# Block pairs of a fused attention and two-MLP kernel: the weight ring moved by 32 bytes, the sums given to VectorE in a new order, and the second token loads issued later

## The chip, the cores and the metric

The kernel runs on one core of a Trainium2 chip. A core has a matrix engine (TensorE, PE in the rows; its weight loads are listed apart as PEld), a vector engine (VectorE, DVE), a scalar engine (ScalarE, ACT), GpSimd (POOL), and SyncE (SP), which here issues all DMA transfers, one after the other in the program's order. The metric is the time of one execution on the device in microseconds (us), as the median of several runs. A change under about 0.2% can't be told from none.

## The reference

Attention is computed twice through 32 packed queries per head, and its output goes through two MLPs. The change touches the second MLP alone.

```python
def _attn_ref(q, k, v, p):
    scale = 1.0 / np.sqrt(q.shape[-1])
    def sm_attn(qq, kk, vv):
        s = scale * np.matmul(qq, kk.transpose(0, 1, 3, 2))
        ...
        return np.matmul(a, vv)
    p_packed = sm_attn(p, k, v)
    return sm_attn(q, p_packed, p_packed)          # 8 x 8 heads, 576 tokens, 64

def _moe_ref(x, w_in, w_out):                      # 4608 x 512, 512 x 2048, 2048 x 512
    h = x @ w_in
    return ((h - np.tanh(h)) @ w_out)

def _moe2_ref(x, w_in, w_out):                     # the same shapes
    h = x @ w_in
    return ((h * np.cos(h)) @ w_out)
```

## The kernel before

A float32 product is made of three reduced-precision products: each operand is split into a `hi` part (rounded by ScalarE) and a `lo` part (the difference, by VectorE), and TensorE computes hi x hi, lo x hi and hi x lo. The result of the first MLP is stored transposed in DRAM as `y1`.

The second MLP works on blocks of 512 tokens (`TB`). The first three are computed plainly (lines 626 and 687). The other six are taken in three pairs (`for t in pairs`, line 1301), and a pair is computed by Strassen-like products of 2x2 blocks: seven products instead of eight, with sums of blocks before and after. A pair has two stages.

- **h blocks.** `F` runs over 8 groups of 256 hidden columns. Each block makes seven products `hprod` (line 883, six matmuls of 512 columns each), with weights of the ring `hw` (`hs.get()`, 8 tiles of 256 KB) and token sums `b` as the moving operand. The names are `B11`, `T1`, `T2`, `B21`, `B22`, `T3`, `T4`. The results stand in three PSUM banks A, C and B of a rotation of four. ScalarE copies intermediate values out (`c1`, `c5`, `c2`), VectorE adds them into `ha` and `hb`, then come rounding, sine and the product with h for the cosine, by `e_round`, `e_frac`, `e_sin`, `e_b2`, `e_a2`, `e_l`, `e_s`, which also leave the operands `K` of the second stage. In the first block of the first pair the weights come from `wf`, tiles that were loaded ahead into another pool. Block F also makes the direct products of block F-1 (`ychunk`): four pieces of six matmuls of 256 columns (line 893), which wait in the list `pend`, and `pop()` issues one piece at a chosen place.
- **Products.** 20 jobs (`jobs`, five kinds `p` in the order `YORDER`, four parts `P` each) of 24 matmuls of 256 columns (line 893): the activations are the weights, and the moving operand is the ring `yw` (5 tiles of 256 KB). For each job ScalarE and VectorE split its operand into `yh` and `yl` (`ysplit`), three jobs ahead. Some operands need a difference of `K` tiles first: `psub`, two per part, 24 in all, on GpSimd. The last job is cut into four pieces that go to `pend` and are issued in the next pair's first blocks.

While the products of a pair run, the token sums of the next pair are prepared by `bprep` (line 815): 26 steps, 13 for each half `j` of the channels. Step 0 and step 13 each load two tiles of 512 KB from `y1` (line 824); the others subtract (line 832, on GpSimd in the pairs), round to `hi` (line 845, 860) and split to `lo` (line 848, 863). The table `PREP` says after which job each step is issued. The loads go into the tiles `gh` and `gl`, two of each, so that the second half's tiles are those of the first half.

The order on each engine is that of the source here (a manual schedule). SP issues the loads of both rings, the token loads and the stores in one queue. A ring load waits for its tile's last matmul, a token load for the last reader of its tile, and everything behind it in the queue waits as well.

Of the kernel before, what the change touches and what calls it, by code (L numbers as in the profile page):

```python
# [10 lines left out]
F32 = mybir.dt.float32  # L11
# [8 lines left out]
ALU = mybir.AluOpType  # L20
# [31 lines left out]
PREP1 = {  # L52
    18: (0,), 19: (1, 2, 5), 20: (3, 4, 13), 21: (6, 7, 8, 9, 14, 15, 18), 22: (10, 16, 17, 19, 20),
    24: (24, 25),
}
# [6 lines left out]
HOPS = ("A11", "S1", "S2", "A12", "S4", "S3", "A22")  # L62
YORDER = (7, 6, 4, 5, 3)
AHEAD = (4, 6)
S4AT = (5, 7, 9, 10)
PREP = {
    0: (0,), 1: (1, 2, 5), 4: (3, 4), 5: (6, 7), 6: (8, 9, 13), 7: (10,), 8: (14, 15, 18), 9: (11, 12),
    10: (16, 17), 11: (19, 20), 12: (21, 22), 13: (23,), 15: (24, 25),
}
SGN = -2147483648  # L70
LOW_BIAS = -0.5 + 2.0 ** -10

# [2 lines left out]
def fused_kernel(ctx, tc, qT, kT, v, pT, w1i, w1o, w2i, w2o, ident, out):  # L75
    nc = tc.nc
    B, _, _, _, HB = qT.shape
# [21 lines left out]
    op = dram.tile([2, 4, 128, DM], F32, name="op")  # L99
# [15 lines left out]
    def f32(ap):  # L115
        return ap.bitcast(F32)
# [10 lines left out]
    class Conv:  # L127
# [47 lines left out]
        def b_ops(self):  # L175
# [5 lines left out]
            def sign():  # L181
                nc.vector.scalar_tensor_tensor(
                    out=x, in0=hi, scalar=SGN, in1=x, op0=ALU.bitwise_and, op1=ALU.bitwise_or
                )
# [448 lines left out]
    def pt2(tag, dt=F32):  # L633
        return p2.tile([128, 2, TB], dt, tag=tag, bufs=2, name=tag)
# [244 lines left out]
    def hprod(dst, w, b, first):  # L879
        n = 0  # L880
        for wi, bi in ((0, 0), (1, 0), (0, 1)):
            for j in range(2):
                nc.tensor.matmul(  # L883
                    out=dst, lhsT=w[:, wi, 128 * j:128 * j + 128], rhs=b[j][bi],
                    start=(first and n == 0), stop=(n == 5), skip_group_check=True,
                )
                n += 1
# [12 lines left out]
    def vec(out, x, y, op=ALU.add):  # L900
        nc.vector.tensor_tensor(out=out, in0=x, in1=y, op=op)  # L901
# [221 lines left out]
    pend, hist, bo, nyt, sums, loaded, evacs = [], [], {}, [], [], [], []  # L1123
# [14 lines left out]
    for n, (i, t, s, a, b) in enumerate(seq):  # L1138
# [9 lines left out]
        for k, x in enumerate(sums):  # L1148
            y = []
# [37 lines left out]
    p4 = p2x["r"]  # L1187
# [14 lines left out]
    def pop(n=1):  # L1202
        for _ in range(n):
            if pend:
                pend.pop(0)()
            while evacs:
                evacs.pop(0)()
# [6 lines left out]
    ha, hb, aa, ab = ea["h"], eb["h"], ea["a"], eb["a"]  # L1214
    spare = [big("ka"), big("kb")]

    banks = [psx.tile([128, TB], F32, tag=f"p{i}", bufs=1, name="p") for i in range(4)]
    nbank = [2]

# [52 lines left out]
    K, kind = {}, {7: 3, 6: 3, 4: 22, 5: 1, 3: 12}  # L1272
# [18 lines left out]

    def ysplit(p, P):
        both = ysplit_lo(*ysplit_hi(p, P))
        if p == 7:
            psub(K[3, P], K[22, P], K[3, P])
        return both

    def psub(o, x, y):
        nc.gpsimd.tensor_tensor(out=o, in0=x, in1=y, op=ALU.subtract)  # L1299

    for t in pairs:
        last = t == pairs[-1]
        Y = {}
        K.clear()

        def e_b2(F):
            vec(ab[:, 0], ab[:, 0], hb[:, 0], ALU.mult)
            vec(ktile(22, F), ab[:, 1], hb[:, 1], ALU.mult)
            vec(ktile(1, F), ktile(22, F), ab[:, 0])

        def e_a2(F, g):
            vec(aa, aa, ha, ALU.mult)
            g["h"], g["l"] = pt2("gh", F32R), pt2("gl", F32R)
            cp(g["h"], aa)
            cp(ktile(12, F), aa[:, 1])

        def e_l(g):
            vec(g["l"], aa, f32(g["h"]), ALU.subtract)

        def e_s(F):  # L1320
            vec(ktile(3, F), aa[:, 0], ab[:, 0], ALU.subtract)

        jobs = [(p, P) for p in YORDER for P in range(NSTEP // 2)]
        done = []
        for F in range(NSTEP):
            w = wfirst if (t, F) == (pairs[0], 0) else None

            def wn(i):
                return w[i] if w else hs.get()

            A, C, B = psp(), psp(), psp()
            c1, c5, c2 = ct("c1"), ct("c5"), ct("c2")
            g = {}
            hprod(A, wn(0), bo["B11"], True)
            hprod(C, wn(1), bo["T1"], True)
            cp(c1, A)
            if F:
                e_sin(eb)
                pop()
            hprod(A, wn(2), bo["T2"], False)  # L1340
            hprod(B, wn(3), bo["B21"], True)
            cp(c5, C)
            if F:
                e_sin(ea)
                e_b2(F - 1)
            cp(c2, A)
            if w:
                for i in PREP1[24]:
                    prep[i]()
            if F:  # L1350
                e_a2(F - 1, g)
            vec(ha[:, 0], B, c1)
            if F:
                e_s(F - 1)
            if F in AHEAD:
                ahead = ysplit_hi(7, len(done))
            hprod(C, wn(4), bo["B22"], False)
            vec(hb[:, 0], C, c2)
            hprod(A, wn(5), bo["T3"], False)
            vec(hb[:, 1], A, c5)  # L1360
            pop(2 if F else 1)
            if F:
                e_l(g)
                while late:
                    late.pop(0)()
                pend.extend(ychunk(Y, F - 1, g["h"], g["l"]))
            put_due()
            hprod(A, wn(6), bo["T4"], False)
            e_round(eb)
            cp(ha[:, 1], A)  # L1370
            if F in AHEAD:
                P = len(done)
                done.append(ysplit_lo(*ahead))
                psub(K[3, P], K[22, P], K[3, P])
            e_round(ea)
            e_frac(eb)
            e_frac(ea)
            pop()
        g = {}
        e_sin(eb)  # L1380
        e_b2(NSTEP - 1)
        e_sin(ea)
        done.append(ysplit(7, 2))
        e_a2(NSTEP - 1, g)
        pop(len(pend))
        e_l(g)
        e_s(NSTEP - 1)
        pend.extend(ychunk(Y, NSTEP - 1, g["h"], g["l"]))
        bo, prep = {}, []
        if not last:  # L1390
            qtags = iter(("gh", "gl", "gh", "gl", "gh", "gl"))
            prep = bprep(
                t + 2, bo, lambda j, nm: pt2(next(qtags)), nc.gpsimd
            )
        Cy = [psp(), psp()]
        for k, (p, P) in enumerate(jobs):
            if k == 3:
                pop(len(pend))
                cp(ha[:, 0], Y["A"][0], TWO_PI)
                cp(ha[:, 1], Y["A"][1], TWO_PI)  # L1400
                plus(ha, Y["B"], ha)
                put(t, 0, 0, ha)
            dst = Y["B"] if p == 3 else Y["A"] if p in (5, 6) else Cy
            hi, lo = done[k]
            fresh = p in (7, 3) and P == 0
            if k == len(jobs) - 1:
                wy = {}

                def tail(half, x, hi=hi, lo=lo, wy=wy, dst=dst):
                    if x not in wy:  # L1410
                        wy[x] = ys.get()
                    yprod(dst, hi[:, x], lo[:, x], wy[x], (2 * half, 2 * half + 1), False)

                def ctail(dst=dst, t=t, o=u2):
                    plus(o, dst, o)
                    put(t, 0, 256, o)

                order = [(h, x) for h in range(2) for x in range(2)]
                pend.extend(lambda h=h, x=x, tail=tail: tail(h, x) for h, x in order)
                late.append(ctail)  # L1420
            else:
                for x in range(2):
                    yprod(dst, hi[:, x], lo[:, x], ys.get(), range(4), fresh and x == 0)
            put_due()
            if len(done) < len(jobs):
                done.append(ysplit(*jobs[len(done)]))
            if k in S4AT:
                i = S4AT.index(k)
                psub(K[12, i], K[12, i], K[3, i])
            if prep:  # L1430
                for i in PREP.get(k, ()):
                    prep[i]()
            if P == NSTEP // 2 - 1:
                if p == 7:
                    cp(hb[:, 0], Cy[0], TWO_PI)
                    cp(hb[:, 1], Cy[1], TWO_PI)
                elif p == 6:
                    cp(aa[:, 0], Y["A"][0], TWO_PI)
                    cp(aa[:, 1], Y["A"][1], TWO_PI)
                elif p == 4:  # L1440
                    plus(aa, Cy, aa)
                    put(t, 1, 0, aa)
                elif p == 5:
                    u2 = [otile(0), otile(1)]
                    cp(u2[0], Y["A"][0], TWO_PI)
                    cp(u2[1], Y["A"][1], TWO_PI)
                    plus(hb, Y["A"], hb)
                    put(t, 1, 256, hb)
# [57 lines left out]
```

## Time and profile before

| | |
|---|---|
| median of 3 runs | 1549.1 us (1548.79 to 1551.68) |
| the profiled execution | 1547.2 us, of which the span from first to last instruction is 1545.2 us |
| TensorE busy | 1478.7 us, 96% of the span |
| VectorE busy | 1216.0 us, 79% |
| ScalarE busy | 976.5 us, 63% |
| GpSimd busy | 250.8 us, 16% |
| mean granted TensorE clock | 0.978 of 2.4 GHz |
| the three pairs | from 1043.6 us on; products end at 1211.9, 1378.2 and 1541.4 us |

The profile lists each instruction with its start and duration, and for idle time before one the instruction that ended it. Matmuls are pipelined: one of 512 columns is listed with 389 ns and the next starts some 230 ns later, so the time from start to start is what it costs. An engine's busy share says little by itself; what counts is where TensorE waits, and for whom.

### The profile page before, as it was taken

How to read it: one execution, taken by the hardware profiler on the slowest of the kernel's cores; microseconds unless marked ns; L12 is line 12 of the kernel's file. 1: busy time of each engine (PE TensorE's matmuls, PEld its weight loads, DVE VectorE, ACT ScalarE, POOL GpSimd, SP SyncE). 2: the span in 40 equal slices, each digit the busy share in tenths (PEclk: the TensorE clock that was granted, in tenths of full speed). 3: DMA queues.
4: the chain of work that ended last, by engine and by line, in shares of the span. 5: the costliest groups of instructions: out<-in, count | busy, mean ns of one | idle time of the engine just before them, and what ended most of it. 6: DMA issues, size and time to landing. Idle time of an engine off the chain costs nothing. (4 is left out here: it accounts for less than half of the span.)

```text
span 1545.2 us, 28227 instructions
## 1 busy us (share of the span) xinstructions
PE 1478.7 (96%) x11056; PEld 1323.5 (86%) x11056; DVE 1216.0 (79%) x1625; ACT 976.5 (63%) x1512; POOL 250.8 (16%) x147
## 2 busy tenths in 40 slices
PE   4879999999999999999999999999998999899999
PEld 1669888999899999989977788888888888898898
DVE  5999888787878878788956558877889578957884
ACT  6878656666656667578867656655665366536652
POOL 1221110010101001011223410000017001630140
PEclk6789999999999999999999999999999999999999
DMA  9523222111112111114658868956666766776656
GB/s 351 190 73 115 82 88 84 47 61 38 60 63 66 63 57 41 48 32 163 200 194 280 278 228 288 356 198 202 188 209 194 215 199 185 219 211 200 181 151 183
DMA packets 149188, 242.56 MB, mean 157 GB/s; under 512 B 12288, under 2 KB 93184, under 8 KB 149056
## 3 DMA queue, kind: packets, MB, share of 16 engines
q1 hardware_dynamic: 149056, 240.76, 48.5%
q8 instruction: 87, 1.43, 0.4%
q14 instruction: 45, 0.37, 0.1%
HBM read 175.44 MB, written 65.27 MB: 156 GB/s over the span
## 5 line engine op out<-in xcount | busy, mean ns | idle before, releaser
L562 PE MATMUL y<-gh,w1o 128*128 128x288 f32 x2048 | 312.1, 305 | 8.0 <-ACT gh L542 3.7
L562 PEld LDWEIGHTS y<-gh,w1o 128*128 128x128 f32 x2048 | 286.2, 192 | 36.4 <-ACT t L515 14.9
L500 PE MATMUL h<-a,g 128*128 128x288 f32 x1536 | 229.2, 298 | 10.3 <-DVE g L481 3.0
L883 PE MATMUL p<-b,hw 128*128 128x512 f32 x966 | 236.7, 396 | 0.3
L500 PEld LDWEIGHTS h<-a,g 128*128 128x128 f32 x1536 | 213.5, 190 | 13.2 <-ACT w1o L226 4.0
L515 ACT ACTIVATE t<-h 128x576 f32<-128x576 f32 x128 | 83.5, 652 | 206.3 <-PE h L500 206.1
L883 PEld LDWEIGHTS p<-b,hw 128*128 128x128 f32 x966 | 177.3, 188 | 39.0 <-DVE hb L901 1.1
L562 PE MATMUL y<-gl,w1o 128*128 128x288 f32 x1024 | 158.1, 296 | 1.2 <-DVE gl L547 1.2
L1299 POOL TENSOR_TENSOR k<-k,k 128x1024 f32<-128x1024 f32 x24 | 79.4, 3322 | 464.3 <-DVE yl L901 442.3
L562 PEld LDWEIGHTS y<-gl,w1o 128*128 128x128 f32 x1024 | 143.6, 189 | 1.6 <-DVE gl L547 1.6
L527 DVE TENSOR_TENSOR t<-h,t 128x576 f32<-128x576 f32 x128 | 95.4, 745 | 59.7 <-ACT u L516 59.6
L626 PE MATMUL h<-yhl,w2i 128*128 128x512 f32 x576 | 134.3, 389 | 0.0
L626 PEld LDWEIGHTS h<-yhl,w2i 128*128 128x128 f32 x576 | 108.1, 188 | 22.4
L534 DVE COPY_PREDICATED y<-k,t 128x576 f32<-128x576 int16 x128 | 107.8, 842 | 12.1 <-ACT t L515 0.5
L547 DVE TENSOR_TENSOR gl<-y,gh 128x576 fp32r<-128x576 f32 x128 | 103.2, 806 | 7.1 <-ACT gh L542 6.2
L893 PE MATMUL y<-yw,yh 128*128 128x256 f32 x576 | 104.4, 282 | 0.1
L530 DVE SCALAR_TENSOR_TENSOR y<-y,d 128x576 f32<-128x576 f32 x128 | 98.2, 767 | 0.0
L687 PE MATMUL y<-w2o,gh 128*128 128x512 f32 x384 | 94.2, 390 | 3.9 <-DVE o L732 2.0
L542 ACT ACTIVATE gh<-y 128x576 fp32r<-128x576 f32 x128 | 87.8, 686 | 15.2 <-DVE y L534 14.6
L901 DVE TENSOR_TENSOR yl<-k,yh 128x1024 fp32r<-128x1024 f32 x54 | 93.5, 1763 | 4.5 <-ACT yh L904 4.1
L528 DVE TENSOR_TENSOR d<-u,h 128x576 f32<-128x576 f32 x128 | 95.0, 742 | 0.0
L893 PEld LDWEIGHTS y<-yw,yh 128*128 128x128 f32 x576 | 89.5, 189 | 1.0 <-ACT o L904 0.2
(162 smaller groups left out, 2693.9 us busy)
## 6 DMA issues: line engine op xcount, KB each, us to landing
yw<-wso SPq DMA_DIRECT2D x96, 256.0 KB, 2.9
hw<-wsi SPq DMA_DIRECT2D x92, 256.0 KB, 3.0
yw<-wod SPq DMA_DIRECT2D x72, 256.0 KB, 3.6
hw<-wid SPq DMA_DIRECT2D x69, 256.0 KB, 3.5
y<-ye SPq DMA_DIRECT2D x80, 144.0 KB, 1.9
st<-w1i SPq DMA_DIRECT2D x16, 512.0 KB, 7.8
v<-vv SPq DMA_DIRECT2D x16, 512.0 KB, 4.8
st<-w1o SPq DMA_DIRECT2D x16, 512.0 KB, 5.7
```

The costliest lines, as they stand in the source:

```text
L500: nc.tensor.matmul(out=h[:, x, 0:HB], lhsT=gw[b, f // 4, half][:, ga, c0:c0 + 128], rhs=a2[b, half][:, aa, HB * j:HB * j + HB], start=(n = ...
L527: lambda: nc.vector.tensor_tensor(out=t, in0=hs, in1=t, op=ALU.subtract),
L528: lambda: nc.vector.tensor_tensor(out=d, in0=u, in1=hs, op=ALU.mult),
L530: lambda: nc.vector.scalar_tensor_tensor(out=y, in0=y, scalar=PC0 - PC1 * PC1 / (4 * PC2), in1=d, op0=ALU.add, op1=ALU.mult,),
L534: lambda: nc.vector.copy_predicated(out=y, mask=k.bitcast(I16), data=t),
L547: nc.vector.tensor_tensor(out=st["gl"], in0=st["g"], in1=f32(st["gh"]), op=ALU.subtract)
L562: nc.tensor.matmul(out=yps[blk][d][:, 0:HB], lhsT=w1out[f][:, wh, 128 * d:128 * d + 128], rhs=st[gg][:, x, :], start=(s in first and x == ...
L626: nc.tensor.matmul(out=h[:, x, :], lhsT=w2in[f][:, wa, 128 * k:128 * k + 128], rhs=yt[k][:, ya, :], start=(n == 0), stop=(n == 11),)
L687: nc.tensor.matmul(out=yps[t, lo_s][m], lhsT=st[gg][:, x, 128 * m:128 * m + 128], rhs=w[:, wh, :], start=(s == lo_s and x == 0 and not lo ...
L883: nc.tensor.matmul(out=dst, lhsT=w[:, wi, 128 * j:128 * j + 128], rhs=b[j][bi], start=(first and n == 0), stop=(n == 5), skip_group_check= ...
L893: nc.tensor.matmul(out=dst[m // 2][:, 256 * (m % 2):256 * (m % 2) + 256], lhsT=src[:, 128 * m:128 * m + 128], rhs=w[:, wi, :], start=(firs ...
L901: nc.vector.tensor_tensor(out=out, in0=x, in1=y, op=op)
```

## The change

It has six parts, all in the block pairs.

1. A tile `pad` of 32 bytes is allocated in the pool of the rings. In the built program it lowers the addresses of `hw`, `yw` and `ab` by 32 bytes (`hw` from 192480 to 192448), to multiples of 64. The copies `c1`, `c5`, `c2` stay where they are.
2. `psub` (all 24 differences of `K` tiles) goes from GpSimd to VectorE, and so do the 16 subtractions of `bprep` in the pairs.
3. The differences are issued at other places: those of K3 in blocks 4 and 6 as before and after jobs 0 and 1; those of K12 in blocks 5 and 7 and after jobs 10 and 14, where all four stood after jobs 5, 7, 9 and 10.
4. `PREP`: the first token load goes from job 0 to 1, the second from job 6 to 10, and the steps between are spread; the last three (`T4` of the second half) move into block 0 of the next pair (`PREP0`).
5. `pop`: two pieces instead of one before the last product of block 0, none at the start and end of block 1 and at the end of block 0, the rest as before, so that from block 2 on each piece is issued one place later.
6. The pieces of the last job take both halves of one weight tile before the second tile, and in the first block of the first pair two products change places.

```diff
-S4AT = (5, 7, 9, 10)
+S4F, S4AT = (5, 7), (10, 14)
 PREP = {
-    0: (0,), 1: (1, 2, 5), 4: (3, 4), 5: (6, 7), 6: (8, 9, 13), 7: (10,), 8: (14, 15, 18), 9: (11, 12),
-    10: (16, 17), 11: (19, 20), 12: (21, 22), 13: (23,), 15: (24, 25),
+    1: (0,), 4: (1, 2), 5: (5, 3), 6: (6, 7), 7: (4, 8), 8: (9,), 9: (10,), 10: (13, 11),
+    12: (12, 14), 13: (15, 18, 16), 14: (19,), 16: (17,), 17: (20, 21), 18: (22,),
 }
+PREP0 = (23, 24, 25)
...
+    pad = p4.tile([128, 8], F32, tag="pad", bufs=1, name="pad")
+    nc.gpsimd.memset(pad, 0.0)
...
     def ysplit(p, P):
         both = ysplit_lo(*ysplit_hi(p, P))
-        if p == 7:
-            psub(K[3, P], K[22, P], K[3, P])
         return both
+    def sum2(P):
+        psub(K[3, P], K[22, P], K[3, P])
+    def sum4(P):
+        psub(K[12, P], K[12, P], K[3, P])
     def psub(o, x, y):
-        nc.gpsimd.tensor_tensor(out=o, in0=x, in1=y, op=ALU.subtract)
+        vec(o, x, y, ALU.subtract)
...
             if F:
                 e_sin(eb)
-                pop()
-            hprod(A, wn(2), bo["T2"], False)
-            hprod(B, wn(3), bo["B21"], True)
+                pop(F > 1)
+            todo = [(A, 2, "T2", False), (B, 3, "B21", True)]
+            for d, i, x, first in reversed(todo) if w else todo:
+                hprod(d, wn(i), bo[x], first)
...
-            if w:
-                for i in PREP1[24]:
+            if F == 0:
+                for i in PREP1[24] if w else PREP0:
                     prep[i]()
...
-            pop(2 if F else 1)
+            pop(2)
...
-                psub(K[3, P], K[22, P], K[3, P])
+                sum2(P)
+            if F in S4F:
+                sum4(S4F.index(F))
             e_round(ea)
             e_frac(eb)
             e_frac(ea)
-            pop()
+            pop(F > 1)
...
-                t + 2, bo, lambda j, nm: pt2(next(qtags)), nc.gpsimd
+                t + 2, bo, lambda j, nm: pt2(next(qtags)), nc.vector
...
-                order = [(h, x) for h in range(2) for x in range(2)]
+                order = [(h, x) for x in range(2) for h in range(2)]
...
+            if k < 2:
+                sum2(2 + k)
             if k in S4AT:
-                i = S4AT.index(k)
-                psub(K[12, i], K[12, i], K[3, i])
+                sum4(2 + S4AT.index(k))
```

On SP, in the products of the first pair, the two tiles of the second token load (`gl` and `gh` from `y_66`, the tensor `y1`) stand among the ring loads `yw`; before, at job 6:

```order
345 L1258 DMA out<-ha 128x2x256 x2
346 L798 DMA yw<-wso_131 128x512
347 L798 DMA yw<-wso_132 128x512
348 L798 DMA yw<-wso_125 128x512
349 L798 DMA yw<-wso_126 128x512
350 L824 DMA gl<-y_66 128x1024
351 L824 DMA gh<-y_66 128x1024
352 L798 DMA yw<-wso_127 128x512
```

and of the change, at job 10:

```order
358 L799 DMA yw<-wso_131 128x512
359 L799 DMA yw<-wso_132 128x512
360 L799 DMA yw<-wso_125 128x512
361 L799 DMA yw<-wso_126 128x512
362 L825 DMA gl<-y_66 128x1024
363 L825 DMA gh<-y_66 128x1024
364 L799 DMA yw<-wso_127 128x512
```

The load stands eight ring tiles, four jobs, further on.

On GpSimd, in the blocks and products of the first pair, before: differences of `K` tiles (`k`, line 1299) and the subtractions of `bprep` (line 832).

```order
95 L1299 TENSOR_TENSOR k_12647<-k_12635,k_12647 128x1024
96 L1299 TENSOR_TENSOR k_12882<-k_12870,k_12882 128x1024
97 L832 TENSOR_TENSOR gh<-gh 128x512
98 L832 TENSOR_TENSOR gh<-gl,gh 128x512 x2
99 L1299 TENSOR_TENSOR k_12178<-k_12178,k_12181 128x1024
100 L1299 TENSOR_TENSOR k_12409<-k_12409,k_12412 128x1024
101 L832 TENSOR_TENSOR gl<-gl,gh 128x512
```

On VectorE, in the products of the first pair of the change, the same work between the splits `yl` (line 902) and the `lo` splits of the token sums (`b`, line 849):

```order
1275 L902 TENSOR_TENSOR yl<-k_12879,yh 128x1024
1276 L902 TENSOR_TENSOR k_12643<-k_12631,k_12643 128x1024
1277 L902 TENSOR_TENSOR yl<-k_12175,yh 128x1024
1278 L902 TENSOR_TENSOR k_12879<-k_12867,k_12879 128x1024
1279 L902 TENSOR_TENSOR yl<-k_12408,yh 128x1024
1280 L1272 SCALAR_TENSOR_TENSOR ha<-y,ha 128x512 x2
1281 L902 TENSOR_TENSOR yl<-k_12643,yh 128x1024
1282 L902 TENSOR_TENSOR yl<-k_12879,yh 128x1024
1283 L833 TENSOR_TENSOR gh<-gh 128x512
1284 L833 TENSOR_TENSOR gh<-gl,gh 128x512
1285 L902 TENSOR_TENSOR yl<-k_12164,yh 128x1024
1286 L833 TENSOR_TENSOR gh<-gl,gh 128x512
```

GpSimd has nothing left in the pairs but the `pad`; VectorE takes a difference between two splits.

## Rows read from the trace of the kernel before

**Rows 1.** Busy time by stage: two h blocks and a product stage of pair two.

```profile
core 0: us, PE busy (x) PEld busy (x) DVE busy (x) ACT busy (x) POOL busy (x), PEclk, DMA share, GB/s
1248.46:1261.10 12.64, 12.64 (x69) 10.76 (x68) 9.38 (x11) 7.89 (x11) 0.00 (x0) 1.00 0.76 219
1261.10:1273.76 12.66, 12.66 (x68) 10.76 (x67) 9.66 (x12) 8.82 (x12) 0.23 (x1) 1.00 0.60 173
1310.60:1378.20 67.60, 62.94 (x505) 62.50 (x504) 55.59 (x40) 34.27 (x40) 35.68 (x14) 0.95 0.70 212
```

**Rows 2.** Waits of the weight loads in the pairs: us in all, times, longest.

```profile
PEld p L893 <- issue: 9.0, 2, 4.8
PEld p L883 <- DVE hb L901: 1.1, 4, 0.3
PEld y L893 <- issue: 1.0, 2, 0.8
PEld y L893 <- DVE gl L901: 0.5, 1, 0.5
```

**Rows 3.** Timeline of TensorE at the two longest waits: start us, us, instruction.

```profile
1177.32 0.28 PE L893 MATMUL p<-yw,yl 128*128 128x256 f32 x1
1181.63 0.77 PE L893 MATMUL p<-yw,yh 128*128 128x256 f32 x2 [4.02 <-DMA yw<-wso]
...
1342.78 0.28 PE L893 MATMUL p<-yw,yl 128*128 128x256 f32 x1
1347.71 0.77 PE L893 MATMUL p<-yw,yh 128*128 128x256 f32 x2 [4.65 <-DMA yw<-wso]
```

**Rows 4.** Busy time in the microseconds after these waits, columns as in rows 1.

```profile
1181.50:1185.00 3.50, 3.37 (x16) 3.40 (x17) 3.50 (x4) 1.36 (x2) 0.85 (x1) 0.52 0.55 209
...
1347.60:1352.00 4.40, 4.29 (x20) 4.32 (x21) 3.69 (x4) 1.35 (x2) 1.76 (x1) 0.50 0.59 183
```

**Rows 5.** Timeline of the SP queue at the first of the two waits.

```profile
1170.80 0.43 SPq L824 DMA_DIRECT2D gl<-y  x1
1176.75 0.32 SPq L824 DMA_DIRECT2D gh<-y  x1
1177.17 2.29 SPq L798 DMA_DIRECT2D yw<-wso  x5
```

**Rows 6.** Timeline of VectorE in the same microseconds.

```profile
1173.30 3.42 DVE L848 TENSOR_TENSOR b<-gh,b 128x1024 fp32r<-128x1024 f32 x1
```

**Rows 7.** Timeline of GpSimd in the same microseconds.

```profile
1168.92 6.72 POOL L1299 TENSOR_TENSOR k<-k,k 128x1024 f32<-128x1024 f32 x2
```

**Rows 8.** Groups of VectorE instructions from 1000 us on: busy us, mean ns of one.

```profile
L901 DVE TENSOR_TENSOR yl<-k,yh 128x1024 fp32r<-128x1024 f32 x54 | 93.5, 1763 | 4.5 <-ACT yh L904 4.1
L910 DVE SCALAR_TENSOR_TENSOR aa<-aa,ha 128x1024 f32<-128x1024 int32 x24 | 39.4, 1643 | 23.7 <-ACT aa L907 23.7
L910 DVE SCALAR_TENSOR_TENSOR ab<-ab,hb 128x1024 f32<-128x1024 int32 x24 | 29.3, 1222 | 2.9 <-ACT ab L907 2.3
L901 DVE TENSOR_TENSOR yl<-ka,yh 128x1024 fp32r<-128x1024 f32 x3 | 3.6, 1213 | 0.0
L832 DVE TENSOR_TENSOR yq<-yq,yt 128x512 f32<-128x512 f32 x2 | 1.4, 684 | 0.0
```

**Rows 9.** Timeline of TensorE in the first block, weights from `wf`.

```profile
1043.63 8.32 PE L883 MATMUL p<-b,wf 128*128 128x512 f32 x36
1051.79 1.07 PE L687 MATMUL y<-w2o,gh 128*128 128x512 f32 x4
```

**Rows 10.** Timeline of TensorE at pair two's first block, weights from `hw`.

```profile
1210.84 0.40 PE L893 MATMUL y<-yw,yh 128*128 128x256 f32 x2
...
1211.92 8.58 PE L883 MATMUL p<-b,hw 128*128 128x512 f32 x36
1220.34 0.41 PE L893 MATMUL y<-yw,yh 128*128 128x256 f32 x2
```

**Rows 11.** Timeline of VectorE in the same block, the last `hb`.

```profile
1220.54 0.69 DVE L901 TENSOR_TENSOR hb<-p,c 128x512 f32<-128x512 f32 x1 [0.66 <-PE p L883]
```

**Rows 12.** DMA issues, 1149.7 to 1155.2 us: KB each, us to landing.

```profile
yw<-wod SPq DMA_DIRECT2D x2, 256.0 KB, 5.5
```

## Prediction

> **What bounds the kernel now.** I read the views in this order: busy shares by stage, the waits of TensorE's weight loads, the timeline of TensorE at the two longest of them, then the SP queue, VectorE and GpSimd in the same microseconds, and last the spacing of the matmuls. The block pairs run from 1043.6 us to the end of the span. In a product stage TensorE is busy for 62.94 of 67.60 us, in one h block (42 matmuls of 512 columns and 24 of 256) for all of its 12.64 us [rows 1]. So TensorE's stream is the bound, and only what shortens it counts: its waits, its clock after a wait, and the time from one matmul to the next.
>
> The waits in the pairs are few. Weight loads idled 9.0 us before line 893 in two places, 1.1 us in four places for `hb`, 1.0 and 0.5 us for a late ring tile and a late `gl` [rows 2]. The two long ones are alike: a matmul starts at 1177.32 and the next at 1181.63, 4.0 us of it idle until `yw` landed; the same at 1342.78 and 1347.71 [rows 3]. For 3.5 and 4.4 us afterwards the granted clock is 0.52 and 0.50, the 1.2 GHz level, and the 16 and 20 matmuls there are busy for 3.37 and 4.29 us [rows 4]. At the normal spacing (0.12 us, below) they take 1.92 and 2.40, so the clock costs 1.45 + 1.89 = 3.3 us.
>
> Why `yw` is late stands in the SP queue: `gl<-y` goes out at 1170.80, `gh<-y` only at 1176.75, and the five ring loads queued behind it at 1177.17 [rows 5]. SP issues in order, and that `gh` tile is still read by the `lo` split of the other channel half, which VectorE runs from 1173.30 to 1176.72, 3.42 us long [rows 6]. It is slow while GpSimd is at two sums of 3.3 us each, from 1168.92 [rows 7].
>
> **What the change does, part by part.**
>
> *Second token loads at job 10 instead of 6.* The last reader of the `gh` tile is the `lo` split at job 6, four jobs (11.5 us) before the load now, and with GpSimd gone it should take 1.2 us, as the uncontended split of the same shape does (1213 ns, [rows 8]). SP should not block. That removes both long waits, 9.0 us, and the slow clock behind them, 3.3 us: **-12.3**. Lower bound of the gain 0, if the wait only moves (a rival).
>
> *Ring at multiples of 64 bytes.* In the built program the pad lowers the tiles `hw`, `yw` and `ab` by 32 bytes; `hw` goes from 192480 to 192448, `c` stays 32 off. TensorE took 36 matmuls on `wf` weights from 1043.63 to 1051.79, 226.7 ns each [rows 9], and 36 of the same shape on `hw` weights from 1211.92 to 1220.34, 233.9 ns each [rows 10]. Same code, same operands but for the weights' tile; `wf` lies at a multiple of 64. DMA traffic does not explain the 7.2 ns: two h blocks with a DMA share of 0.76 and 0.60 take 12.64 and 12.66 us [rows 1]. 966 matmuls on `hw` at 7 ns: 6.8 us at most, 0 if it is not the address. I take **-6.6**, the row being nearly the direct measure. For `yw` as moving operand I take nothing: nine matmuls of 256 columns take 1.08 us, 120 ns each [rows 10]; 512 columns at one a cycle of 2.4 GHz are 213.3 ns, which leaves 13.4 ns of the aligned 226.7 for each matmul, and 256 columns so come to 120.1 ns. The other end, half of 226.7 for 256 columns, would be 113.3 and 6.7 ns less for each of 24 x 84 = 2016 such matmuls, 13.5 us; I take the end that the cycle count meets.
> By the Trainium skill (SBUF — State Buffer, section Specifications), SBUF lines are 16 bytes, so a tile 32 bytes off still starts on a line and would cost nothing. By that rule the term is 0 and the sum 6.6 us smaller; no run shows yet which of the two holds, and the rival below prices it.
>
> *Sums from GpSimd to VectorE.* 24 sums of 128x1024 and 16 of 128x512 leave GpSimd, where two of the large take 6.72 us [rows 7]. On VectorE the nearest rows are 1213 ns and 684 ns [rows 8]: 24 x 1.21 + 16 x 0.68 = 40 us more. What goes: 54 splits at 1763 ns against 1213 for the same shape without GpSimd at work, 29.7 us, and 24 roundings at 1643 against 1222, 10.1 us [rows 8]. VectorE's total stays about even. It must fit where it lands. In a product stage VectorE is busy 55.59 of 67.60 us, GpSimd's delays included; in an h block 9.38 of 12.64 us [rows 1]; the fullest new block adds a split (1.2) and a sum (1.2): 11.8 us, under the 12.4 us that TensorE needs at aligned spacing (42 x 226.7 ns + 24 x 120 ns). So I cost it at nothing; the cover is the 0.6 us left in those blocks, and in the product stage splits made three jobs (8.6 us) ahead of use. If the cover is gone, each sum costs up to its 1.2 us.
>
> *Pops.* Line 883 waits for `hb` at the first two blocks of pairs two and three, because one piece of 0.72 us (the last 256-column products, 6 x 120 ns) stands between the last reader of A and the product that overwrites it, while `hb` takes 0.69 us from 1220.54 on [rows 11], and the piece began at 1220.34 [rows 10]. With two pieces there (1.44 us) it is covered: four waits, -1.1. The late `gl` (0.5) was a piece popped right after it was made, and is now popped a step later. In return the first two starts of block 1 have no piece in front: A is copied by ScalarE with only C's 1.36 us as cover, and `hb` of block 1 comes about as late as the two pieces last. The nearest price is the 0.27 us of one `hb` wait; three pairs with one or two such: 0 to +1.6, I take +1.0.
>
> *First load after the weights.* The first token load now goes out behind the two `yw<-wod` tiles of the last chunk; these took 5.5 us to land behind it [rows 12], and the 1.0 us wait above is theirs: -1.0, to be paid again in part by the ring loads that now stand behind both loads, +0.5.
>
> *The rest:* the T4 ops moved into block 0 (about 2 us in three steps over two engines) wait at most for a copy of the third product and are needed after the sixth and two pieces, 3 x 1.36 + 1.44 = 5.5 us later; the reordered tail ends with the same last matmul; the memset has nothing behind it on GpSimd. 0.
>
> **Sum:** -12.3 - 6.6 - 1.1 - 0.5 - 1.0 + 1.0 + 0.5 = -20.0 us. The profiled execution took 1547.2 us around its span of 1545.2, 1.9 us (0.12%) under the median of 1549.1. From the median: 1529.1 us; I say **1529**. With every gain and no new wait it is 21.5 to 22: 1527.
>
> **Rivals.**
>
> *A, the address is not it.* The 7 ns could belong to something else that sets `hw` apart, such as where in SBUF the ring lies, which hardly moves. For: no other weights of the trace lie there. Against: no DMA or stage dependence. Without the term: 1549.1 - 13.4 = 1535.7 us. The line size on the skill's page of SBUF would give this.
>
> *B, the ring starves elsewhere.* Both second loads now go out together, 1 MB, at job 10, just ahead of the stores of `aa`. Ring tiles issued behind 1 MB took 5.5 us [rows 12], where a tile is used four products (5.8 us) after its slot is free, so there is 0.3 us to spare. Were VectorE also late with the `lo` split at job 6 by more than four jobs, SP would block as now. Price: one to two waits of 1 to 4 us, with slow clock when long: +4 to +12, 1533 to 1541 us.
>
> *C, slower: VectorE becomes the bound.* If a block's VectorE work passes 12.4 us, or its splits come later than three jobs, every sum and difference lies on the path: 40 - 20 = +20, 1569 us; it decides from 0.6 us more per fullest block. For: block waits show VectorE handing `hb` over just in time. Against: the 11.8 us above, and the roundings that get shorter.
> The Trainium skill (Perfetto Trace Analysis, section Optimizing Scalar/DVE Operations) says that a saturated DVE is a reason to offload to other engines, GpSimd too, and adds that the two share a port, so that it may not help. This case takes the work back; the rows show the shared cost (1763 against 1213 ns) but no saturation.
>
> *D, nothing changes:* the pad might not move the ring or SP's order might be kept; the built program's addresses and rows exclude both.
>
> **How the numbers follow.** A change of 0.2% (3.1 us) is about what timing this kernel can tell from none. Chances: the forecast 0.72, A 0.11, B 0.12, C 0.03, other 0.02. Forecast, A and most of B end over 3.1 us faster: faster 0.95, same 0.02, slower 0.03. Range: from every gain and some of `yw` as well, 1525, to A and the lower half of B, 1537.
>
> **What would show it.** Right: no TensorE wait over 1 us in the pairs and no 0.5 clock there; 36 matmuls on `hw` in 8.16 us; h blocks of 12.40 us instead of 12.65; GpSimd idle in the pairs and the splits at 1.2 us; `gh<-y` issued within a microsecond of `gl<-y`. Wrong: `hw` spacing still near 234 ns (A); waits for `yw` after job 10 (B); TensorE waiting for `yl`, `gl` or `hb` in blocks 4 to 7 or at the first jobs (C).

## The result and the profile after

The changed kernel takes 1529.1 us (median of 4 runs, 1528.2 to 1530.6), before 1548.9 (4 runs, 1547.7 to 1551.7): a ratio of 0.9871 with a 95% interval of 0.9854 to 0.9888. The forecast was 1529. The time is right, but one of its terms is not: the 6.6 us that the ring's address was to give on `hw` did not come, and 5.1 us that the text had set at nothing came in their place.

| | before | after |
|---|---|---|
| profiled execution, span | 1547.2, 1545.2 us | 1528.2, 1526.1 us |
| GpSimd busy | 250.8 us | 140.2 us |
| VectorE busy | 1216.0 us | 1201.5 us |
| mean granted clock | 0.978 | 0.994 |
| first h product to the last matmul's start | 497.5 us | 478.7 us |

The last row, called the stretch of the pairs below, is worked out from the start times of the matmuls of lines 883 and 893 (884 and 894 after). It leaves out what follows the last matmul and what lies ahead of the pairs, whose start differs by up to 2.5 us between the profiles of this study (1042.5 to 1045.0 us).

Busy time by stage after, pair two: the two h blocks that answer to those of [rows 1], the next one, which has the most work for VectorE, and the product stage (columns as in [rows 1]):

```profile
1238.23:1250.85 12.62, 12.62 (x68) 10.71 (x67) 9.38 (x11) 7.88 (x11) 0.00 (x0) 1.00 0.80 234
1250.85:1263.48 12.63, 12.63 (x68) 10.71 (x67) 9.61 (x12) 8.84 (x12) 0.00 (x0) 1.00 0.63 188
1263.48:1276.11 12.63, 12.63 (x69) 10.72 (x67) 11.60 (x14) 7.90 (x11) 0.00 (x0) 1.00 0.65 186
1301.36:1361.74 60.38, 59.84 (x507) 59.49 (x505) 48.92 (x51) 33.03 (x39) 0.00 (x0) 1.00 0.78 238
```

The product stage lost the long wait and the slow clock (0.95 before, 1.00 now). The h block is 12.63 us long where 12.40 was expected: the first sign that `hw` did not get faster. All waits of weight loads in the pairs that the view lists after (columns as in [rows 2]):

```profile
PEld p L894 <- issue: 1.3, 2, 0.7
PEld y L894 <- issue: 0.4, 2, 0.2
```

Where 9.0 us stood for line 893 there are 1.3, and the waits for `hb` and `gl` are gone. The SP queue shows why (start us, us, instruction; compare [rows 5]):

```profile
1168.44 11.20 SPq L799 DMA_DIRECT2D yw<-wso  x9
1179.69 0.43 SPq L825 DMA_DIRECT2D gl<-y  x1
1180.17 0.42 SPq L825 DMA_DIRECT2D gh<-y  x1
1180.69 4.39 SPq L799 DMA_DIRECT2D yw<-wso  x4
```

`gh<-y` goes out 0.48 us behind `gl<-y` and the ring loads 0.5 us later; before, 5.95 us lay between the two. On VectorE the splits have their uncontended length (groups, columns as in [rows 8]):

```profile
L902 DVE TENSOR_TENSOR yl<-k,yh 128x1024 fp32r<-128x1024 f32 x54 | 65.4, 1219 | 19.0 <-ACT yh L905 18.6
L911 DVE SCALAR_TENSOR_TENSOR aa<-aa,ha 128x1024 f32<-128x1024 int32 x24 | 29.4, 1224 | 16.4 <-ACT aa L908 16.4
L902 DVE TENSOR_TENSOR k<-k,k 128x1024 f32<-128x1024 f32 x24 | 29.3, 1219 | 0.2
```

1763 ns became 1219 and 1643 became 1224; 28.1 and 10.0 us are given back, 29.3 go to the differences and 10.9 to the 16 subtractions of `bprep`; the other splits (`gl`, `b`) got shorter too, so that VectorE's total fell. The timeline of TensorE after shows the spacing (start us, us, instruction; the pieces of [rows 10], and a product job from 1165.86 on):

```profile
1165.86 0.39 PE L894 MATMUL y<-yw,yh 128*128 128x256 f32 x2
...
1171.64 0.39 PE L894 MATMUL y<-yw,yh 128*128 128x256 f32 x2
...
1201.76 0.40 PE L894 MATMUL y<-yw,yh 128*128 128x256 f32 x2
...
1202.82 0.40 PE L894 MATMUL y<-yw,yh 128*128 128x256 f32 x2
...
1203.17 8.56 PE L884 MATMUL p<-b,hw 128*128 128x512 f32 x36
1211.58 0.40 PE L894 MATMUL y<-yw,yh 128*128 128x256 f32 x2
```

36 products on `hw` still take 8.41 us, 233.6 ns each (233.9 before). But 9 matmuls of 256 columns take 1.06 us from 1201.76 on, 117.8 ns each, where nine took 1.08 before [rows 10], and 51 of them from 1165.86 to 1171.64 only 113.3 ns.

### The profile page after: what moved, and what is told of

Same layout as the page of the kernel before. It is cut to its first block, busy times and chain, and to the rows that moved or that the text cites. A ratio compares the mean times of both kernels' runs of the same rounds, so it can differ in the third digit from the quotient of the medians.

```text
span 1526.1 us, 28182 instructions
## 1 busy us (share of the span) xinstructions
PE 1469.5 (96%) x11056; PEld 1314.3 (86%) x11056; DVE 1201.5 (79%) x1665; ACT 975.4 (64%) x1512; POOL 140.2 (9%) x108
## 5 line engine op out<-in xcount | busy, mean ns | idle before, releaser
L535 DVE COPY_PREDICATED y<-k,t 128x576 f32<-128x576 int16 x128 | 107.9, 843 | 12.1 <-ACT t L516 0.5
L688 PEld LDWEIGHTS y<-w2o,gh 128*128 128x128 f32 x384 | 73.0, 191 | 20.5 <-DVE o L733 2.9
L523 ACT ACTIVATE y<-u 128x576 f32<-128x576 f32 x128 | 87.6, 684 | 0.1
```

Source lines behind the costliest of these rows:

```text
L535: lambda: nc.vector.copy_predicated(out=y, mask=k.bitcast(I16), data=t),
L688: nc.tensor.matmul(out=yps[t, lo_s][m], lhsT=st[gg][:, x, 128 * m:128 * m + 128], rhs=w[:, wh, :], start=(s == lo_s and x == 0 and not lo ...
```

## The experiments

Spacings in the table below are means of the time from one matmul's start to the next, over the 966 products on `hw` and the 576 matmuls `p<-yw` of the product stages, waits and slow clock left out. "Off" is the address of the tiles modulo 128, from the built programs. The 116.9 ns of the changed kernel are the mean of jobs at 117.8 and some ten at 113.3, which come and go (last section), so a difference of 1 ns between two rows of that column need not be the offset's.

| kernel | `hw` off | `yw` off | `hw` 512 columns, ns | 256 columns, ns | steady h block, us | stretch of the pairs, us |
|---|---|---|---|---|---|---|
| before | 96 | 96 | 233.4 | 120.0 | 12.66 | 497.5 |
| changed | 64 | 64 | 233.4 | 116.9 | 12.63 | 478.7 |
| e1, before with the pad | 64 | 64 | 233.4 | 117.4 | 12.63 | 498.7 |
| e2 | 32 | 32 | 233.6 | 116.9 | 12.61 | 480.3 |
| e3 | 0 | 0 | 228.3 | 120.0 | 12.46 | 478.2 |
| e4 | 0 | 0 | 228.3 | 120.0 | 12.46 | 479.4 |
| e5 | 0 | 64 | 228.6 | 117.8 | 12.45 | 476.0 |
| e6 | 64 | 0 | 229.4 | 120.0 | 12.49 | 479.9 |
| e11 | 0 | 32 | 228.1 | 116.7 | 12.40 | 475.3 |

### The pad alone, and other pads

**e1: the kernel before, with only the 32-byte pad.**

```diff
+    pad = p4.tile([128, 8], F32, tag="pad", bufs=1, name="pad")
+    nc.gpsimd.memset(pad, 0.0)
```

> The kernel before with the 32-byte tile alone. Theory (the address shift is worth the spacing of the 256-column matmuls that take yw as moving operand, and nothing for the weights hw): mean spacing of line 893 near 117.5 ns where it is 119.7 before, hw still 233.4 ns, both long waits kept: 5 us less, 1544. Rival (the shift does nothing by itself; the shorter 256-column spacing came with VectorE's work or the pops): 119.7 ns, 1549.

Measured: 1546.2 us, ratio 0.9987 (0.9979 to 0.9996), so 2.0 us, not 5. The spacing came as expected (117.4 and 233.4 ns), and the products on `hw` gained nothing. The profiled run took 1548.2 us, and its stretch is even 1.2 us longer than before: in it all of the gain was lost. What ate the gain is in the timeline of TensorE in e1:

```profile
1175.67 0.28 PE L893 MATMUL p<-yw,yl 128*128 128x256 f32 x1
1181.74 0.77 PE L893 MATMUL p<-yw,yh 128*128 128x256 f32 x2 [5.79 <-DMA yw<-wso]
```

TensorE came to the wait 1.65 us earlier than before [rows 3], but the tile landed no earlier: it idles 5.79 us where it idled 4.02, and in pair two 5.53 for 4.65. The slow clock afterwards was longer too, 26 and 29 matmuls where it was 16 and 20 (busy time in the microseconds after the two waits, as in [rows 4]):

```profile
1181.60:1187.30 5.70, 5.56 (x26) 5.59 (x27) 3.27 (x4) 0.93 (x1) 3.41 (x2) 0.50 0.48 158
1348.30:1354.60 6.30, 6.16 (x29) 6.20 (x30) 3.54 (x4) 1.42 (x3) 3.74 (x3) 0.50 0.46 154
```

**e2, e3, e4: the changed kernel with pads of 64, 96 and 1888 bytes.**

```diff
-    pad = p4.tile([128, 8], F32, tag="pad", bufs=1, name="pad")
+    pad = p4.tile([128, 16], F32, tag="pad", bufs=1, name="pad")      # e2; 24 in e3, 472 in e4
```

> The changed kernel with a pad of 64 bytes instead of 32, so the ring tiles move but stand 32 bytes off multiples of 64 as before the change. Theory (the offset in 64 bytes counts): 256-column spacing back at 119.7 ns, 1534. Rival (it is where the ring lies, or that the rest of the change made the spacing shorter): 117.5 ns, 1529.

> The changed kernel with a pad of 96 bytes: ring tiles at multiples of 128, as wf, w2i, w2o, gh and gl all are. Theory (hw is slow because 64 is not enough): hw spacing 226.7 ns, 6.5 us less, and the 256-column spacing down too, at most to 106.7 to 113 ns (up to 8 to 20 us less): 1502 to 1522. Rival (hw is slow for something else than its offset): 233.4 ns, 1529.

> The changed kernel with a pad of 1888 bytes: ring tiles 128 bytes behind multiples of 2048, exactly as the tiles wf. Theory (multiples of 128 are what counts): the same as with 96 bytes. Rival 1 (a larger period counts): faster here than with 96 bytes, hw at 226.7 ns only here. Rival 2 (not the offset): hw 233.4 ns in both, 1529.

Measured: e2 1530.1 us (one run), 116.9 ns. So 32 bytes off a multiple of 64 is not slow by itself; that theory is wrong. Of the three offsets away from 128 only the 96 bytes of before show 120.0 ns. e3 took 1530.1 us (ratio 0.9883, 0.9868 to 0.9898), e4 1530.1 (0.9880, 0.9867 to 0.9894): no change in time, and two changes in the spacing that cancel. `hw` got to 228.3 ns, most of the way to the 226.7 of the theory, and the 256-column matmuls went back to 120.0, which no theory had. The timeline of TensorE in e3:

```profile
1203.55 0.40 PE L894 MATMUL y<-yw,yh 128*128 128x256 f32 x2
...
1204.27 0.40 PE L894 MATMUL y<-yw,yh 128*128 128x256 f32 x2
...
1204.63 8.35 PE L884 MATMUL p<-b,hw 128*128 128x512 f32 x36
1212.82 0.40 PE L894 MATMUL y<-yw,yh 128*128 128x256 f32 x2
```

36 products in 8.19 us, 227.5 ns each; six of 256 columns in 0.72 us, 120.0 each. e4, at the tiles' place modulo 2048 of `wf`, does the same (228.3 and 120.0): a larger period does not show. Both kernels put the rings 128 bytes off a multiple of 256, so a period of 256 was not told apart.

**e5, e6: the two rings at offsets of their own**, by a second pad between them.

```diff
     hs.fill()
+    pad2 = p4.tile([128, 16], F32, tag="pad2", bufs=1, name="pad2")
+    nc.gpsimd.memset(pad2, 0.0)
     ys.fill(2)
...
-    pad = p4.tile([128, 8], ...)      # kept in e5
+    pad = p4.tile([128, 24], ...)     # e6
```

> The changed kernel with a second pad of 64 bytes between the two rings: hw at multiples of 128, yw as in the change (64 bytes off them). Theory (each operand's own offset counts, weights want 0 and the moving operand wants not 0): hw 227 to 228 ns as with the 96-byte pad, 256-column matmuls 117.5 ns as in the change, h blocks 12.35 to 12.4 us, 5 to 6.5 us less than the change: 1523 to 1524. Rival (the spacing goes by the two rings together, or 256-column matmuls are slow whenever hw is fast): 120 ns, 1529.

> The changed kernel with the offsets the other way about: hw 64 bytes off multiples of 128, yw at multiples of 128. Theory (each operand's own offset counts): hw 233.4 ns, 256-column matmuls 120.0 ns, 5 us more than the change: 1534. Rival (the two rings together): not both of these.

Measured: e5 1526.1 us (ratio 0.9869, 0.9849 to 0.9889), one run of e6 1529.8. In e5 both operands are at a better value, 228.6 and 117.8 ns, and the stretch of the pairs is 2.7 us shorter than in the change, where the theory had 5 to 6.5: of the 4.7 us that `hw` gives 1.4 go to longer waits for ring tiles, and fewer jobs are at 113.3 ns. The ratio can't tell 2.7 us apart. e6 speaks against "each its own offset": with `hw` 64 bytes off as in the change, its products are at 229.4 ns as soon as `yw` stands at multiples of 128. For `hw` one of the two at a multiple of 128 is nearly enough; the 256-column matmuls go by `yw`.

**e11: `hw` at multiples of 128, `yw` 32 bytes behind them.**

```diff
-    pad = p4.tile([128, 8], ...)
+    pad = p4.tile([128, 16], ...)
     hs.fill()
+    pad2 = p4.tile([128, 8], ...)
     ys.fill(2)
```

> The changed kernel with hw at multiples of 128 and yw 32 bytes behind them. Theory (hw as in the kernels with hw at 128; 256-column matmuls near 116.8 ns as with the 64-byte pad, where yw stood 32 bytes behind a multiple of 128): hw 228 to 229 ns, 0 to 1.4 us less than with yw 64 bytes behind: 1525 to 1526. Rival (the offsets work together in no simple sum): some other pair of spacings, 1526 to 1530.

Measured: 1523.8 us, ratio 0.9841 (0.9826 to 0.9855), the fastest of all. Busy time in two of its h blocks:

```profile
1239.04:1251.44 12.40, 12.40 (x68) 10.69 (x67) 9.38 (x11) 7.89 (x11) 0.00 (x0) 1.00 0.76 235
1251.44:1263.84 12.40, 12.40 (x68) 10.69 (x67) 9.58 (x12) 8.83 (x12) 0.00 (x0) 1.00 0.64 192
```

These are the 12.40 us that the prediction had for the change, though by other spacings (228.1 and 116.7 ns, where it took 226.7 and 120). Of the 5.1 us on `hw` (966 times 5.3 ns) 2.7 are lost again to waits for ring tiles, 4.7 us in this profile, with the matmul behind each, and 2.0 in that of the change. Its interval touches that of the change.

### The second token load

**e7: the kernel before, with the table of steps of the change alone** (`PREP` and `PREP0` as in the change).

```diff
-    0: (0,), 1: (1, 2, 5), 4: (3, 4), 5: (6, 7), 6: (8, 9, 13), ...
+    1: (0,), 4: (1, 2), 5: (5, 3), 6: (6, 7), 7: (4, 8), 8: (9,), 9: (10,), 10: (13, 11), ...
+PREP0 = (23, 24, 25)
```

> The kernel before with the new places of the token steps alone (second load at job 10, last three steps in block 0); sums stay on GpSimd, no pad, old pops. Theory (the later load takes the two long waits away, whoever makes the sums): both waits and the slow clock behind them gone, 12.3 us less, 1537. Rival (GpSimd's delay of the split is what matters, and the wait only moves): a wait of 2 us or more for yw behind job 10, 1541 to 1549.

Measured: 1534.9 us, ratio 0.9922 (0.9906 to 0.9937), 12.1 us less. Both long waits are gone (the longest of a weight load in the pairs is 1.4 us) and the clock stays at full speed, with GpSimd still at the sums. The timeline of the SP queue in e7:

```profile
1183.64 0.43 SPq L825 DMA_DIRECT2D gl<-y  x1
1184.12 0.42 SPq L825 DMA_DIRECT2D gh<-y  x1
1184.64 7.72 SPq L799 DMA_DIRECT2D yw<-wso  x6
```

`gh<-y` goes out 0.48 us behind `gl<-y`, though the `lo` split of the first half is still slow here (3.31 us, from 1173.88 on). The new table without the other parts is enough. That it is the later load in it, and not another of the moved steps, follows from this queue and was not tried by itself.

**e8: the changed kernel with the load at job 7.**

```diff
-    ... 7: (4, 8), 8: (9,), 9: (10,), 10: (13, 11),
+    ... 7: (13, 4, 8), 8: (9,), 9: (10,), 10: (11,),
```

> The changed kernel with the second token load at job 7 instead of 10, one job behind the split of the tile that it overwrites, as it was before the change. Theory A (with the sums off GpSimd that split takes 1.2 us and is done in time): no wait over 1 us, 1529 to 1531. Theory B (the distance of four jobs is what keeps SP from blocking): SP blocks on gh<-y by 2 us or more and TensorE waits for yw twice, 4 to 6 us each with slow clock behind: 1537 to 1541.

Measured: 1531.4 us, ratio 0.9898 (0.9883 to 0.9914). The timeline of the SP queue in e8:

```profile
1172.74 0.42 SPq L825 DMA_DIRECT2D gl<-y  x1
1173.26 0.38 SPq L825 DMA_DIRECT2D gh<-y  x1
1173.78 7.53 SPq L799 DMA_DIRECT2D yw<-wso  x6
```

SP does not block. The longest wait is one of 1.2 us for a ring tile, a little over the 1 us of theory A, which so holds in the main; the 4 to 6 us of theory B did not come. With the split at 1.22 us one job of distance will do. So the later load (e7, e9) and the sums on VectorE (e8) are each enough for the long waits, and their gains don't add. The sums on VectorE with all the old places were not tried.

**e12: e7 with the 32-byte pad**, two parts of the change.

```diff
+    pad = p4.tile([128, 8], F32, tag="pad", bufs=1, name="pad")
```

> The kernel before with two parts of the change, the new places of the token steps and the 32-byte pad. Theory (the shorter 256-column spacing was eaten by the two long waits when the pad was tried alone, since what they wait for does not come sooner; without these waits it is worth its full 5 us): 4.5 to 5 us less than the token steps alone, 1530, ratio to before near 0.989. Rival (other waits of the product stages eat it as well): 1532 to 1535.

Measured: 1534.3 us, ratio 0.9909 (0.9892 to 0.9925). Against e7 that is 2.0 us by the ratios, whose intervals overlap, and 2.7 by the stretch of the pairs (487.0 to 484.3). The 256-column matmuls gave 3.8 us, and waits for `yl` and `yw` took 1.1 back. The time is in the rival's range and the gain about half of the theory's; how much of the spacing is paid out with GpSimd still at work stays open.

### The sums and the pops

**e9: the changed kernel with the sums on GpSimd.**

```diff
-        vec(o, x, y, ALU.subtract)
+        nc.gpsimd.tensor_tensor(out=o, in0=x, in1=y, op=ALU.subtract)
...
-                t + 2, bo, lambda j, nm: pt2(next(qtags)), nc.vector
+                t + 2, bo, lambda j, nm: pt2(next(qtags)), nc.gpsimd
```

> The changed kernel with the 24 differences of K and the subtractions of the token sums back on GpSimd, at the changed places. Theory (VectorE has room either way; the later load alone ends the long waits): yl splits back near 1.7 us, no wait of TensorE over 1.5 us, the same to 2 us more than the change: 1529 to 1531. Rival 1 (taking GpSimd out is what ends the waits): waits of 4 us for yw in the products, 1537 to 1541. Rival 2 (the sums on VectorE cost time on the path): faster than the change, 1520 to 1527.

Measured: 1540.4 us, ratio 0.9947 (0.9932 to 0.9962), 11 us more than the change; none of the three had this. There is no long wait for `yw`, but a new one of 1.36 us in six h blocks, those with `F` 5 and 7 in each pair. The timeline of VectorE in one of them (start us, us, instruction):

```profile
1268.28 1.22 DVE L911 SCALAR_TENSOR_TENSOR ab<-ab,hb 128x1024 f32<-128x1024 int32 x1
1269.94 2.90 DVE L911 SCALAR_TENSOR_TENSOR aa<-aa,ha 128x1024 f32<-128x1024 int32 x1 [0.45 <-ACT aa L908]
1272.77 2.89 DVE L902 TENSOR_TENSOR ab<-ab,hb 128x512 f32<-128x512 f32 x1
```

The timeline of GpSimd in the same microseconds:

```profile
1268.51 6.60 POOL L1307 TENSOR_TENSOR k<-k,k 128x1024 f32<-128x1024 f32 x2 [60.72 <-DVE yl L902]
```

The timeline of TensorE at the end of it:

```profile
1279.12 0.28 PE L894 MATMUL y<-yw,gl 128*128 128x256 f32 x1
1280.77 1.67 PE L884 MATMUL p<-b,hw 128*128 128x512 f32 x6 [1.37 <-DVE hb L902]
```

Busy time in this block (columns as in [rows 1]):

```profile
1268.72:1282.97 14.25, 12.88 (x68) 10.78 (x67) 13.61 (x12) 7.89 (x11) 6.31 (x2) 1.00 0.57 176
```

While GpSimd is at two sums (6.60 us), two instructions of VectorE take 2.90 and 2.89 us where 1.22 and 0.69 are usual, 3.9 us more. VectorE's twelve instructions so come to 13.61 us, more than the 12.63 us that the block takes without a wait, and it hands `hb` over late. With the sums on VectorE the same block has fourteen instructions in 11.60 us (third row of the first view above). Six such waits are 8.2 us, 9.8 with the slower matmuls around them, and ring tiles 2 more. The Trainium skill (SBUF — State Buffer, section Who interferes with whom) says that a VectorE instruction with both inputs in SBUF contends with a GpSimd instruction that reads SBUF. By that rule both instructions here, which read `aa` and `ha`, `ab` and `hb`, contend with the sums, and the rows agree.

**e10: the changed kernel with the pops of before.**

```diff
-                pop(F > 1)
+                pop()
...
-            pop(2)
+            pop(2 if F else 1)
...
-            pop(F > 1)
+            pop()
```

> The changed kernel with the pops of before. Theory (the pops are worth their waits): the waits for hb at the first two blocks of pairs two and three are back, four of 0.3 us with the slow matmul behind each, and the one for gl of 0.4 to 0.5 us: 1.9 us more than the change, 1531. Rival (the order of the T4 steps or VectorE's work moved these waits): none of them back, 1529.

Measured: one run, 1533.7 us. Weight loads wait as the theory said (columns as in [rows 2]):

```profile
PEld p L884 <- DVE hb L902: 1.1, 4, 0.3
...
PEld y L894 <- DVE gl L902: 0.5, 1, 0.5
```

With the slower matmul behind each that is 1.9 us. The stretch of the pairs is 3.8 us longer than in the profile of the change; another 1.4 of these are ring waits, which vary between runs, and 0.5 the product jobs (117.8 against 116.9 ns). A further 1.8 us lie behind the last matmul, which this single run does not explain.

## Why the prediction was right, and where it was not

Step by step, by the stretch of the pairs (497.5 to 478.7 us, 18.8 less):

| step | predicted | measured |
|---|---|---|
| two long waits and the slow clock behind them | -12.3 | -12.4 |
| waits for `hb`; for `gl` | -1.1; -0.5 | -1.4; -0.5 |
| `yw<-wod` behind the first load | -1.0 | -1.1 |
| starts of block 1 | +1.0 | 0 |
| ring loads behind the first load | +0.5 | +1.4 |
| other short waits | 0 | +0.3 |
| products on `hw` | -6.6 | +0.1 |
| 256-column matmuls on `yw` | 0 | -5.1 |

*The long waits.* Right in cause and size. e7 and e8 add what the text had not said: either of the two, the later load or the split's 1.2 us, is enough. The four jobs of slack and the 1.2 us split were counted as one mechanism; they are two.

*Ring at multiples of 64 bytes.* This step failed, in both its sentences. The row of `wf` was taken as "aligned to 64" and showed 226.7 ns; but `wf` stands at a multiple of 128, and 64 bytes off gives `hw` nothing (233.4 ns before, in e1 and after). That e3 and e4 bring 228.3 ns shows that the address does matter, so rival A, which had it that the address is not the cause, was wrong as well, though its term of 0 was right for `hw`. Its neighbour, "for `yw` I take nothing", rested on counting 256 columns at one a cycle with a fixed part left over. The other end that the text gave, 113.3 ns, is the spacing of part of the product jobs after the change. The two errors, 6.7 and 5.1 us, nearly cancelled. That the time was met to the microsecond is luck: of the 18.8 us some 13.7 were understood and 5.1 were not.
The Trainium skill's rule cited there (SBUF — State Buffer, section Specifications) has 16-byte lines, by which neither a shift of 32 bytes nor one of 64 costs anything. The runs disagree: 228.3 against 233.4 ns, and 116.7 against 120.0.

*Sums on VectorE.* Costed at nothing, and right for the reason given: 11.60 us busy in a fullest block, 11.8 predicted, and no wait for `yl` there. What the step did not see is the other side: with GpSimd at the new places the kernel would be 11 us slower (e9). The sums had to go to VectorE for the new order, where rival C had asked whether VectorE could bear them.

*Pops and first load.* The four waits and the late `gl` went, and e10 brings them back. Block 1 starts without a wait. The ring tile behind the first load waits 0.62 and 0.66 us in two pairs, with 0.07 each behind it, more than the 0.5 taken; in other kernels of the same order this wait is 0.3 to 1.9 us.

Rival B did not come: behind the second load TensorE waits 0.2 us for a ring tile in two pairs, not 1 to 4. Neither did C and D.

## What to carry to other kernels

Take the time from start to start of equal matmuls apart by the tiles they read, and compare address offsets before a gain is booked: a row that is fast shows that its own offset is good (here a multiple of 128), not which weaker condition would do. A faster engine in front of a wait for something else gives its gain back to that wait (e1: 5 us of spacing, 2 us of time), so remove the wait first. And a sum that agrees is no proof of its terms: read each from the trace after.

## What the runs showed that was not expected

From one matmul to the next the spacing varies by some ns (116 to 124 in the kernel before), but its mean over a job keeps to a few values: 120.0, 117.8, 116.7 and 113.3 ns for 256 columns, the last half of the 226.7 for 512. With `yw` 64 bytes off 128, jobs are at 117.8 and now and then at 113.3 for up to ten in a row; no run shows what starts or ends these. With `yw` 32 bytes off they are mostly at 116.7 (some twenty jobs of e2 at 117.8), at multiples of 128 always at 120.0. The better offset for the weights of the long products is thus the worse one for the short ones that move `yw`. In e3 the products that follow a piece run through a fixed pattern and then settle (two products, ns from start to start):

```
233 236 228 233 231 226 227 227 226 227 227 226
```

The 226.7 ns at which they settle so become 228.3 in the mean. The Trainium skill (SBUF — State Buffer, section Who interferes with whom) gives TensorE one read port for the moving operand and an independent one for the weights. That does not explain the runs: from the change to e6 the products on `hw` went from 233.4 to 229.4 ns though `hw` keeps its offset modulo 128 and these products do not read `yw`, the ring whose offset changed; the pieces between them do. The offset of `b`, which they read as moving operand, was never varied. No run here shows what inside TensorE or SBUF ties the spacing to the offsets, or why 96 bytes off 128 differs from 32; that stays open.
